# A ninth loop round that a branch ends early, and an output ring of 292 columns, in a grouped 1x1 convolution

## The chip, the cores and the metric

The kernel runs on one core of one Trainium2 chip. The metric is device time in microseconds (us) of that core, lower is better. Runs of one kernel mostly agree within 0.3%, so differences need several runs and are given here with medians, ratios and 95% intervals.

## The reference

The input `x` is 512 x 512 pixels of 192 channels in bf16, in 4 groups of 48 channels; each group is multiplied by its own 48 x 48 matrix.

```python
def reference(x, w):                       # k = 1, G = 4, Cg = 48
    xg = xp.reshape(B, H + 2 * pad, W + 2 * pad, G, Cg)
    ...
            out = out + jnp.einsum('bhwgc,gcd->bhwgd', xg[:, i:i+H, j:j+W, :, :], w[i, j])
    return out.reshape(B, H, W, C)
```

About 100.7 MB are read and 100.7 MB written, and the arithmetic per byte is small.

## The kernel before

Pixels lie along 128 partitions; a "column" is one pixel of each partition (384 bytes a partition). The SP queue loads columns into an input ring of 3 slots of 80 columns. TensorE (PE) transposes 4 columns at a time (a "group"), VectorE copies the transposed data to SBUF, PE multiplies with the block weights, ScalarE (ACT) casts the result into an output ring, and ACT's queue stores parts of that ring. Two groups make a "pair". There are 514 groups, 257 pairs.

The sizes and the cutting of the output ring into stores:

```python
RCOLS = SLOTS * BIG                  # 240
OGRID = (72, 144, 216, 288)          # where a store ends in the output ring
OCOLS = OGRID[-1]
LATE_COLS = 240                      # near the end: parts of 44 ...
LATE_PART = 44
LAST_PARTS = (12, 32, 16, 8)         # ... and these for the last stores
# cut
```

PE's program has a loop. Its body is 30 pairs, because buffer addresses and semaphores repeat after 60 groups. What does not divide by 30 is straight code ahead of the loop:

```python
def loop_spans(units):
    body, out, run = RCOLS // 4, [], []
    # cut
            first = max((run[0].g0 - 1) // 2, 1)                            # 9
            rounds, rest = divmod(run[-1].g1 - 2 * first - 2, body)         # 8, 14
            if rounds > 1:
                out.append((first + rest // 2, body // 2, rounds))          # (16, 30, 8)
# cut
            for first, body, rounds in LOOPS:
                for pair in range(pair, first):      # 16 pairs of straight code
                    step(pair)
                with pe.Fori(0, rounds):             # 8 rounds of 30 pairs
                    for pair in range(first, first + body):
                        step(pair)
                pair = first + rounds * body
            for pair in range(pair, NP):             # one pair more
                step(pair)
```

ACT copies a group into the output ring once the store that last used its columns has landed (`landed` below), and issues a store when its last group is done:

```python
            for g in range(NG):
                act.wait_ge(mm_done, g + 1)
                while todo and stores[todo[0]].g1 <= g - 1:
                    issue(todo.pop(0))
                if over[g] is not None:
                    landed(over[g])
                # cut: the copy
```

Two "special fields" of 48 columns are written to leave some of the 16 DMA engines out, or to give them less, to even out their work (in the trace of before, the load of such a transfer over 4 engines has one early semaphore update, at 84.9 us, and then four landings, at 107.9 to 110.9 us; a full load has 16):

```python
PARTIAL = (                                   # queue, first row, rows, engines, columns less
    ("sync", 0, 16, 4, 0), ("sync", 32, 16, 4, 0),
    ("pool", 52, 44, 11, 0), ("pool", 20, 12, 3, 0), ("pool", 96, 32, 8, 0),
)
UNEVEN = (("sync", 0, 16, 4, 16), *PARTIAL[1:])
FRONT = ((6, ((48, PARTIAL), (32, FULL))), (11, ((48, UNEVEN), (32, FULL))))
```

## Time and profile before

| | before |
|---|---|
| time, first three runs | 477.03 to 477.23 us, median 477.2 |
| span of the profiled run | 475.5 us |
| DMA from 32 to 436 us | 431 GB/s, share 1.00 |
| bytes moved | 201.57 MB |
| ACT's waits for stores | 17.7 us, nine times |
| PE's instruction fetches (queue q8) | 9 packets, 0.15 MB |

This is the view of windows. Each line has a stretch in us and its length, the busy time of each engine with its count of instructions, the granted PE clock, the mean busy share of the 16 DMA engines, and GB/s:

```profile
28.00:32.00 4.00, 3.97 (x63) 3.69 (x62) 2.12 (x3) 3.65 (x6) 0.00 (x0) 1.00 1.02 344
32.00:436.00 404.00, 375.20 (x5463) 339.43 (x5461) 217.74 (x228) 342.79 (x455) 11.19 (x20) 0.99 1.00 431
436.00:464.00 28.00, 26.30 (x379) 23.12 (x376) 14.99 (x16) 25.03 (x34) 0.00 (x0) 1.00 1.00 426
464.00:475.50 11.50, 0.00 (x0) 0.00 (x0) 0.00 (x0) 0.76 (x1) 0.00 (x0) 0.63 0.71 299
```

From 32 to 464 us the DMA engines have, on the average of each stretch, no free time. In that time no compute engine is busy throughout: PE has 375 us of work in 404, ACT 343. At 431 GB/s the 201.57 MB alone need 467.7 us of the 475.5 us. The last stretch still moves data, though PE is done and ACT has one copy left.

The page's lines of the DMA queues (packets, MB, share of the 16 engines' span) show where the bytes go: q1 loads, q10 stores, q0 the GpSimd transfers, q8 and q14 instructions:

```profile
q1 hardware_dynamic: 4320, 97.44, 48.0%
q10 hardware_dynamic: 4976, 97.42, 47.9%
q0 software_dynamic: 1216, 6.49, 3.3%
q8 instruction: 9, 0.15, 0.1%
q14 instruction: 9, 0.07, 0.0%
```

The source view of the loop's line shows its branches; the columns are the count and then the shortest, median and longest duration in ns:

```profile
L392 PEldq ALU_OP  x8: 36/36/42, 85.7 to 461.5; - x8
L392 PEldq COMPARE_BRANCH  x8: 76/208/239, 85.8 to 461.6; - x8
```

The view of waits shows ACT waiting for stores to leave the output ring (total us, times, longest):

```profile
ACT oring L446 <- DMA out_dram<-oring: 17.7, 9, 3.9
```

And the end of the timeline (start us, us, engine, line) shows ACT's last copy and its last two store issues; the span ends more than 10 us later:

```profile
463.58 0.34 ACTq L427 DMA_DIRECT2D out_dram<-oring  x1
463.96 0.80 ACT L446 CAST oring<-o_ps 128x768 bf16<-128x768 f32 x1 [0.28 <-issue]
464.79 0.34 ACTq L427 DMA_DIRECT2D out_dram<-oring  x1
```

### The profile page before, as it was taken

Reading aid. Unit: us, or ns where it says so; the run is one execution under the profiler, and the core shown is the slowest. Engines: PE = TensorE matmul, PEld = TensorE weight load, DVE = VectorE, ACT = ScalarE, POOL = GpSimd, SP = SyncE. Lnnn points to the kernel's source line nnn. Section 1 sums busy time; section 2 is a strip of 40 time slices with the busy share of each in tenths; the row PEclk is TensorE's granted clock in tenths of the full one; section 3 lists DMA queues with packets and bytes.
Section 4 is the critical chain, followed back from the end, with each engine's and each line's share of the span. In section 5 each row is a group of like instructions: output and inputs, shape, how many; then the busy total and the mean of one; then the engine's idle time right before and its main releaser. Section 6 shows DMA issues by size and latency. Waiting matters only on the chain.

```text
span 475.5 us, 13580 instructions
## 1 busy us (share of the span) xinstructions
PE 427.4 (90%) x6178; PEld 386.3 (81%) x6178; DVE 246.8 (52%) x258; ACT 388.9 (82%) x515; POOL 12.5 (3%) x28
## 2 busy tenths in 40 slices
PE   5999999999698999999999897999698988999990
PEld 4988888888597988888888786888697877888870
DVE  2555565555354555555555543655354554555540
ACT  2899899998587998999998795898687868998890
POOL 1000000200002000000000000200002000000000
PEclk9999999999999999999999998999989999999996
DMA  8999999999999999999999999999999999999997
GB/s 326 439 393 421 435 426 429 442 416 433 435 434 428 435 421 435 435 429 435 429 434 432 430 432 430 432 430 428 433 433 428 433 429 427 428 435 428 423 429 307
DMA packets 10530, 201.57 MB, mean 424 GB/s; under 512 B 2096, under 2 KB 2096, under 8 KB 2608
## 3 DMA queue, kind: packets, MB, share of 16 engines
q1 hardware_dynamic: 4320, 97.44, 48.0%
q10 hardware_dynamic: 4976, 97.42, 47.9%
q0 software_dynamic: 1216, 6.49, 3.3%
q8 instruction: 9, 0.15, 0.1%
q14 instruction: 9, 0.07, 0.0%
HBM read 100.68 MB, written 100.66 MB: 423 GB/s over the span
## 4 chain that ended last, share of the span: by engine, by line
PE 61%; DMA 19%; ACT 12%; another core or an unknown queue 3%; issue 2%; ACTq 1%; SPq 0%; POOLq 0%
PE o_ps L370 35%; PE xT_ps L350 26%; ACT oring L446 12%; DMA out_dram<-oring 10%; DMA ring<-in_x_dram 9%; ACTq L427 1%; SPq L320 0%; SPq L313 0%; ACTq L420 0%; POOLq L300 0%; POOLq L299 0%; ACTq L429 0%
## 5 line engine op out<-in xcount | busy, mean ns | idle before, releaser
L446 ACT CAST oring<-o_ps 128x768 bf16<-128x768 f32 x514 | 387.6, 801 | 75.1 <-PE o_ps L370 47.0
L409 DVE COPY xT_sb<-xT_ps 128x1536 bf16<-128x1536 bf16 x257 | 246.1, 958 | 211.9 <-PE xT_ps L350 211.9
L370 PE MATMUL o_ps<-wt,xT_sb 128*128 128x144 bf16 (+1 forms) x3084 | 288.4, 235 | 25.1 <-ACT oring L446 20.6
L370 PEld LDWEIGHTS o_ps<-wt,xT_sb 128*128 128x128 bf16 x3084 | 211.6, 99 | 63.3 <-ACT oring L446 55.0
L350 PE MATMUL xT_ps<-ident,ring 128*128 128x128 bf16 x3084 | 220.4, 221 | 8.4 <-POOLq L300 4.3
L350 PEld LDWEIGHTS xT_ps<-ident,ring 128*128 128x128 bf16 x3084 | 188.3, 99 | 11.3 <-POOLq L300 4.5
L286 POOL DMA_DIRECT2D fill<-in_x_dram x8 | 4.6, 573 | 350.2 <-PE xT_ps L350 231.6
L296 POOL DMA_DIRECT2D ring<-in_x_dram x6 | 3.3, 560 | 0.0
L307 POOL DMA_DIRECT2D out_dram<-oring x6 | 3.3, 556 | 0.0
L332 PE MATMUL o_ps<-w_sb,esel 48*128 48x48 bf16 x10 | 0.6, 209 | 2.6 <-DMA w_sb<-in_w_dram 2.6
L332 PEld LDWEIGHTS o_ps<-w_sb,esel 48*128 48x128 bf16 x10 | 0.4, 111 | 2.5 <-POOL esel L273 2.5
L402 DVE CAST wt<-o_ps 128x480 bf16<-128x480 f32 x1 | 0.7, 657 | 3.2 <-PE o_ps L332 3.2
L446 ACT ACT_TABLE_LOAD x1 | 1.3, 1283 | 0.8 <-PEq L466 0.8
L273 POOL TENSOR_SCALAR_AFFINE_SELECT esel<-esel 48x272 bf16<-48x272 bf16 x1 | 0.4, 402 | 0.0
L270 POOL MEMSET esel<- 48x272 bf16 x1 | 0.3, 318 | 0.3 <-POOLq L466 0.3
L277 POOL TENSOR_SCALAR_AFFINE_SELECT ident<-ident 128x128 bf16<-128x128 bf16 x1 | 0.3, 282 | 0.0
L271 POOL MEMSET ident<- 128x128 bf16 x1 | 0.2, 198 | 0.0
L466 POOL MEMSET const-float32-0.0<- 128x1 f32 x1 | 0.1, 98 | 0.3 <-issue 0.3
L466 POOL MEMSET const-bfloat16-1.0<- 128x1 bf16 x1 | 0.1, 101 | 0.0
L466 POOL MEMSET const-uint8-127<- 128x1 uint8 x1 | 0.1, 101 | 0.0
L466 POOL MEMSET const-float32-1.0<- 128x1 f32 x1 | 0.1, 98 | 0.0
## 6 DMA issues: line engine op xcount, KB each, us to landing
ring<-in_x_dram SPq DMA_DIRECT2D x22, 3840.0 KB, 29.0
out_dram<-oring ACTq DMA_DIRECT2D x21, 3456.0 KB, 42.6
out_dram<-oring ACTq DMA_DIRECT2D x3, 2112.0 KB, 20.6
out_dram<-oring ACTq DMA_DIRECT2D x3, 1536.0 KB, 34.8
ring<-in_x_dram SPq DMA_DIRECT2D x2, 1536.0 KB, 35.0
out_dram<-oring ACTq DMA_DIRECT2D x1, 3072.0 KB, 37.9
out_dram<-oring ACTq DMA_DIRECT2D x1, 2688.0 KB, 37.5
ring<-in_x_dram SPq DMA_DIRECT2D x1, 2688.0 KB, 25.4
```

Of the source, the lines that this page charges most:

```text
L273: gp.affine_select(out=esel[:], in_=esel[:], pattern=[[-1, ECOLS]], compare_op=AluOpType.is_equal, fill=0.0, base=ESHIFT, channel_multipli ...
L286: gp.dma_start(dst, src).then_inc(fill_sem[k], 16)
L296: gp.dma_start(sbuf, dram).then_inc(ld_sem[ld_key[p.i, n]], 16)
L307: gp.dma_start(dram, sbuf).then_inc(st_sem[i][n], 16)
L332: last = pe.matmul(o_ps[:, NOB - 1, col:col + CG], lhsT=esel[:, s0:s0 + 128], rhs=w_sb[:, g, :], start=True, stop=True, skip_group_check=True)
L350: last = pe.transpose(xT_ps[:, g % NXP, j * 128:(j + 1) * 128], xg[:, j * 128:(j + 1) * 128], ident[:])
L370: last = pe.matmul(o_ps[:, v % NOB, c0_:c1_], lhsT=xs[:, j * 128:(j + 1) * 128], rhs=wt[:, WOFF[tc]:WOFF[tc] + (c1_ - c0_)], start=(tc == ...
L402: dve.tensor_copy(wt[:], o_ps[:, NOB - 1, 0:WCOLS]).then_inc(wc_sem, 1)
L409: dve.tensor_copy(xT_sb[pair % NXS][:, 0:n * 2 * UC].rearrange("p (g c) -> p g c", g=n), xT_ps[:, b0:b0 + n, 0:2 * UC]).then_inc(e_done[pa ...
L427: act.dma_start(dram, sbuf).then_inc(st_sem[i][n], 16)
L446: act.copy(out_columns(g).rearrange("p (u c) -> p u c", u=2), o_ps[:, v % NOB:v % NOB + 2, 0:UC]).then_inc(fa_done[g % (2 * NTOK)] if g < ...
L466: nc = _bacc.Bacc("TRN2", target_bir_lowering=False, num_devices=1)
```

## The change

The changed kernel is called after. The intent is twofold. PE's program gets shorter: the seven pairs that do not divide by 30 are run as a ninth round of the loop, which a branch leaves after those seven. And the output ring gets 4 columns longer, with one part of 76 columns among parts of 72.

```diff
-OGRID = (72, 144, 216, 288)
+OGRID = (72, 144, 220, 292)
-LAST_PARTS = (12, 32, 16, 8)
+LAST_PARTS = (32, 16, 12, 8)
...
-                out.append((first + rest // 2, body // 2, rounds))
+                out.append((first, body // 2, rounds, rest // 2))
...
-            for first, body, rounds in LOOPS:
+            for first, body, rounds, rest in LOOPS:
                 for pair in range(pair, first):
                     step(pair)
-                with pe.Fori(0, rounds):
-                    for pair in range(first, first + body):
+                with pe.Fori(0, rounds + 1) as i:
+                    for pair in range(first, first + rest):
                         step(pair)
-                pair = first + rounds * body
+                    with pe.If(i < rounds):
+                        for pair in range(first + rest, first + body):
+                            step(pair)
+                pair = first + rounds * body + rest
```

## The prediction

> **What bounds the kernel now.** The DMA engines. By the view of windows the core moves 431 GB/s at a share of 1.00 from 32 to 436 us and 426 GB/s from 436 to 464 us. The page's 201.57 MB at 431 GB/s are 467.7 us of the 475.5 us span. The rest (about 8 us) is the start, a dip to 344 GB/s from 28 to 32 us, and the tail: ScalarE's last copy ends at 464.8 us and 10 us of stores still drain. [...]
>
> The compute engines have slack. A pair of groups takes about 1.65 us in undisturbed stretches of the timeline, so 257 pairs need about 424 us (estimate). ScalarE waits 17.7 us, nine times, for stores to free the output ring, but at a DMA share of 1.00 that only shows that bytes are queued.
>
> **What the change does.**
> 1. Loop: before, 16 pairs of straight code, 8 rounds of 30 pairs, one pair. After, 9 pairs, 8 rounds of 30, a ninth of 7 that a branch leaves, one pair: the same 257 pairs. PE's static code shrinks by 7 pairs of 48 instructions, 336 of about 2,290. Fetches were 9 packets of 16 KB (page, instruction queue q8), each about 0.94 us on one DMA engine in the trace's records; I expect 7 or 8. [...] This trace has 8 loop branches of about 0.21 us (source view), and no PE fetch after 89 us, so the 30-pair body stays resident; I expect no refetch. Added: nine branches of 0.1 to 0.25 us, hidden behind PE's slack.
> 2. Ring of 292 columns with a part of 76: 36 stores before and after, same bytes. ScalarE's 17.7 us of store waits should shrink by a few us at most; the DMA queue is full anyway, so nothing of that reaches the end.
> 3. Last parts 32, 16, 12, 8 instead of 12, 32, 16, 8: the tail is a backlog draining one store after another (the last three land at 472.2, 474.1 and 475.0 us), at the same rate in any order. Under 0.3 us.
>
> **What is left.** In the last store, the slowest DMA engine finishes 1.7 us after the median one and 0.9 us after the next. If that engine also carries PE's fetches, two fewer give at most about 0.9 us; otherwise their mean is 0.1 us. I expect part of it.
>
> **Predicted time:** 476.7 us, 8 in 10 between 475.5 and 477.7. Faster by over 2%: 0.01; within 2%: 0.97; slower by over 2%: 0.02.
>
> **What would show each step.** DMA share still 1.00 and 431 GB/s in the middle; q8 at 7 or 8 packets with none late in the run; 9 more compare-and-branches with no gap at PE around them; store waits a little shorter; a tail of about 10 us.
>
> **What would make it wrong.** [...] If the shifted stores change how the 16 DMA engines drift apart, the end moves by 1 to 2 us either way.

Three passages are cut, where marked. The forecast's sum is 477.2 us, the median of before's first three runs, less 0.5 us for the two fetches: 476.7 us. Three of its figures are estimates: 0.1 to 0.25 us for a branch (the trace of before has seven of 207 to 239 ns and one of 76 ns), under 0.3 us for the last parts, and 1 to 2 us for shifted stores (in before's last store the last engine is 0.9 us behind the next and 1.7 us behind the median).

## The result, and the profile after

| | before | after |
|---|---|---|
| median of 6 runs | 477.28 us (477.03 to 478.10) | 476.38 us (476.04 to 477.45) |
| ratio | | 0.998, interval 0.9967 to 0.9993 |
| span of the profiled run | 475.5 us | 474.6 us |

A ratio in this document is the mean time of one kernel's fast runs over the mean of the other's in the same rounds, so it is not quite the ratio of the medians. The kernel is 0.9 us faster, well within 2%, but the interval excludes 1. The predicted 476.7 us was 0.3 us too high and the range 475.5 to 477.7 us holds the result.

The lines of after that answer to those shown of before. The windows:

```profile
28.00:32.00 4.00, 3.97 (x61) 3.60 (x59) 2.39 (x3) 3.45 (x6) 0.00 (x0) 1.00 0.92 349
32.00:436.00 404.00, 375.77 (x5448) 339.27 (x5445) 217.18 (x228) 341.78 (x454) 11.17 (x20) 0.98 1.00 431
436.00:464.00 28.00, 26.02 (x375) 22.89 (x373) 15.09 (x16) 24.02 (x33) 0.00 (x0) 1.00 1.00 426
464.00:475.50 11.50, 0.59 (x6) 0.38 (x6) 0.00 (x0) 1.59 (x2) 0.00 (x0) 0.69 0.69 290
```

The middle is the same to the last digit: 431 GB/s at share 1.00, then 426. The gain is not there.

The two queues whose packets matter are q10 and q8; q0 stands between them on the page:

```profile
q10 hardware_dynamic: 4976, 97.42, 47.9%
q0 software_dynamic: 1216, 6.49, 3.3%
q8 instruction: 7, 0.11, 0.1%
```

PE's fetches went from 9 packets to 7, and the stores kept their 4976 packets. The branches, from the source views of two lines, first the loop's own and then the one that leaves the ninth round:

```profile
L393 PEldq COMPARE_BRANCH  x9: 76/208/225, 73.8 to 462.2; - x9
```

```profile
L396 PEldq COMPARE_BRANCH  x9: 77/77/208, 35.1 to 461.8; - x9
```

There are ten branches more, one of them the loop's end for the ninth round. The new ones take 77 ns (84 ns in the first two rounds) where they fall through, that is, where PE goes on with the next instruction, and 208 ns the one time they are taken. The loop's own branch jumps back seven times in before and eight times in after; its last one, of 76 ns, falls through. ACT's waits for stores, and the end:

```profile
ACT oring L450 <- DMA out_dram<-oring: 13.9, 7, 3.9
```

```profile
464.62 0.34 ACTq L431 DMA_DIRECT2D out_dram<-oring  x1
465.00 0.80 ACT L450 CAST oring<-o_ps 128x768 bf16<-128x768 f32 x1 [0.21 <-issue]
465.83 0.34 ACTq L431 DMA_DIRECT2D out_dram<-oring  x1
```

ACT waits 3.8 us less for the ring. But it finishes 1.0 us later than before (its last copy ends at 465.80 against 464.76 us), and yet the span ends 0.9 us earlier. So the end is not set by ACT: it is the tail of DMA work that got shorter.

How that tail ends can be read from the trace's semaphore updates, which no view of the page prints. Each full store's semaphore gets 16 updates at different times; they are read here as one from each DMA engine, when its share has landed. The trace doesn't name the engine. These are the 16 landings of the last store, in us from the span's start:

```
before  468.1 470.6 470.8 472.1 472.1 473.1 473.2 473.3 473.3 473.3 473.4 473.5 473.7 473.7 474.1 475.0
after   468.3 470.2 470.9 471.7 472.0 472.0 472.2 473.0 473.1 473.1 473.2 473.2 473.6 473.8 473.9 474.1
```

The mean of the 16 moves by only 0.3 us (472.7 to 472.4). The last one moves by 0.9 us, and that is the gain: before, one engine came 0.9 us behind all the others; after, none does.

### The profile page after: what moved, and what is told of

Read it like the earlier page. It is cut to its first block, busy times and chain, and to the rows that moved or that the text cites. A ratio compares the mean times of both kernels' runs of the same rounds, so it can differ in the third digit from the quotient of the medians.

```text
span 474.6 us, 13600 instructions
## 1 busy us (share of the span) xinstructions
PE 428.2 (90%) x6178; PEld 386.2 (81%) x6178; DVE 246.8 (52%) x258; ACT 388.4 (82%) x515; POOL 12.5 (3%) x28
## 3 DMA queue, kind: packets, MB, share of 16 engines
q10 hardware_dynamic: 4976, 97.42, 47.9%
## 4 chain that ended last, share of the span: by engine, by line
PE 63%; DMA 20%; ACT 10%; another core or an unknown queue 2%; issue 1%; ACTq 1%; SPq 0%; POOLq 0%
PE o_ps L371 37%; PE xT_ps L351 27%; DMA out_dram<-oring 11%; ACT oring L450 10%; DMA ring<-in_x_dram 10%; ACTq L431 1%; SPq L321 0%; SPq L314 0%; ACTq L424 0%; POOLq L301 0%; POOLq L300 0%; ACTq L433 0%
```

## The experiments

Twelve kernels ran, and before ran in the same rounds. Two theories stood at the start. Theory F: the gain is the two fetches of PE code that are no longer made, one of them from the engine that ends last. Theory S: the gain is the stores' new cutting (ring and last parts), which shifts how the engines drift apart.

### One part alone: e1_loop, e2_ringlast, e3_ring

e1_loop is after with the ring and parts of before:

```diff
-OGRID = (72, 144, 220, 292)
+OGRID = (72, 144, 216, 288)
-LAST_PARTS = (32, 16, 12, 8)
+LAST_PARTS = (12, 32, 16, 8)
```

> The loop change alone, with the old ring of 288 and the old last parts. Theory F (the gain is the two instruction fetches that PE no longer makes): 7 packets on queue q8 instead of 9, and most of the 0.9 us: 0.5 to 1.0 us faster than before. Theory S (the gain comes from the stores' new cuts, that is ring and last parts): within 0.2 us of before, though q8 has 7 packets.

e2_ringlast is before with the ring and the parts of after, and e3_ring is before with the ring alone:

```diff
-OGRID = (72, 144, 216, 288)
+OGRID = (72, 144, 220, 292)
-LAST_PARTS = (12, 32, 16, 8)        # this line in e2_ringlast only
+LAST_PARTS = (32, 16, 12, 8)
```

> The ring of 292 and the new last parts, with the old loop (16 straight pairs, 8 rounds). Theory F: within 0.2 us of before, q8 at 9 packets. Theory S: 0.5 to 1.0 us faster than before, with q8 at 9. If both parts count, each of the two runs shows about half.

> The ring of 292 alone, with the old last parts, which then need a 37th store because one of them crosses the ring's end. Theory F: within 0.2 us of before. Theory S with the ring as its cause: as e2_ringlast. Theory S with the last parts as its cause: within 0.2 us of before or slower by a few tenths (one store more).

| kernel | fetches (q8) | median us | ratio to before | interval |
|---|---|---|---|---|
| before, same rounds | 9 | 477.34 | | |
| e1_loop | 7 | 476.32 | 0.9982 | 0.9968 to 0.9996 |
| e2_ringlast | 9 | 477.03 | 0.9993 | 0.9979 to 1.0006 |
| e3_ring | 9 | 477.25 | 0.9999 | 0.9986 to 1.0013 |

The loop alone brings 1.0 us, which is all of the change's gain. The ring and parts without the loop are not clear of zero; an effect of up to 0.3 us, as e2_ringlast's median has it, can't be told from noise here. In e2_ringlast's last store one engine still lands last and alone, at 474.9 us with the next at 474.0. e3_ring shows why ring and last parts were changed together: with the old parts the new ring needs a 37th store, because one part crosses the ring's end (q10 then has 5120 packets in place of 4976). ACT's waits for stores fell to 13.0 us in e3_ring:

```profile
ACT oring L446 <- DMA out_dram<-oring: 13.0, 6, 4.0
```

That is 4.7 us less waiting than before at the same time within noise: here, with the queue full anyway, taking the wait away gained nothing. How much of the waits is the ring's doing is less clear, because they move without it too: e1_loop, with the old ring, has 15.3 us of them, e2_ringlast 16.5.

### What a fetch costs: e4_code4

Four of the eight rounds of before are unrolled ahead of the loop. The work is the same, the code is longer by 120 pairs:

```diff
-                out.append((first + rest // 2, body // 2, rounds))
+                out.append((first + rest // 2 + 4 * (body // 2), body // 2, rounds - 4))
```

> The kernel before with 4 of the 8 rounds unrolled ahead of the loop: 120 pairs of straight code more, 5,760 PE instructions, about 22 more fetches of 16 KB at about 0.95 us each on one DMA engine; nothing else changes. Theory F: q8 at about 31 packets; if they all sit on the engine that ends last, up to 21 us slower; if two engines share them, about 10 us; if all sixteen share them, 1.3 us. Theory S: no matter where they sit, they would cost less than 0.3 us, since a fetch is small beside the 201 MB.

```profile
q8 instruction: 31, 0.51, 0.4%
```

It took 480.33 us at the median, ratio 1.0064 (1.0050 to 1.0077): 3.0 us slower than before. Theory S had allowed 0.3 us. None of theory F's own figures (21, 10 or 1.3 us, for one, two or sixteen engines) fits either. The 22 fetches carry 0.36 MB, which at 431 GB/s spread over all engines would be 0.8 us. In the last store eight engines stand apart:

```
e4_code4  473.1 473.1 473.2 473.2 473.2 473.2 473.3 473.7 475.9 477.4 477.7 477.8 477.9 478.0 478.2 479.0
```

Eight land by 473.7 us, one at 475.9, seven at 477.4 or later. 31 fetches dealt out in turn to eight engines are four for seven of them and three for the eighth. That gave theory R: the fetches go round eight of the sixteen DMA engines, and the engine with most fetches sets the end. Nine fetches are then one too many: eight engines have one each, and the ninth gives one of them a second.

The packets themselves can be checked. The trace does not name a packet's engine, but in before 99.6% of the packets of 512 bytes or more that start between 32 and 436 us have another packet that starts 3 to 4 ns before their recorded end, and each of the nine fetches has one that starts 13 to 15 ns before its end. Such pairs are read here as one engine's work, and packets are linked end to start. Where two engines end within a few ns a link is ambiguous, and a chain may hop to another engine there, so a single chain is evidence and no proof. In before, the chain of packets that carries the first fetch (at 18.2 us) goes on from its end at 19.2 us and reaches the ninth (at 89.1 us); the eight fetches up to 79.9 us lie on eight different chains.

### The staircase: e5_f8, e6_f9, e7_f16, e8_f17

The form of the new loop allows any number of fetches: pairs can be moved ahead of the loop, with the ninth round shorter in return. These four are e1_loop with 3, 7, 45 and 51 such pairs:

```diff
             first = max((run[0].g0 - 1) // 2, 1)
+            first += 3                 # 7 in e6_f9, 45 in e7_f16, 51 in e8_f17
             rounds, rest = divmod(run[-1].g1 - 2 * first - 2, body)
```

> The loop change of e1_loop with 3 more pairs of straight code ahead of the loop (12 instead of 9; the ninth round leaves after 4 pairs): 8 fetches of PE code. Theory R (the fetches go round eight DMA engines in turn, so the ninth is the first that gives an engine a second one, and the end is set by the engine with most fetches): q8 at 8 packets and as fast as e1_loop, 0.8 to 1.1 us faster than before. Rival P (each fetch costs its share, about 0.14 us by e4_code4's 3.0 us for 22, wherever it sits): half of e1_loop's gain, 0.4 to 0.6 us.

> The same with 7 more pairs (16 straight pairs as before, the ninth round leaves at once, the branch stands at the head of the loop): 9 fetches. Theory R: the gain is gone, within 0.3 us of before, though the kernel has the new loop and branch. Rival B (the gain comes from the branch or the loop's new place, not from fetches): 0.7 to 1.1 us faster than before.

> The same with 45 more pairs (54 straight pairs, 6 full rounds and one that leaves): 16 fetches, two for each of eight engines. Theory R: as e6_f9 and before, within 0.4 us of before. Rival P: 7 fetches more than before, 0.9 to 1.0 us slower than before.

> The same with 51 more pairs (60 straight pairs): 17 fetches, so that one engine gets a third. Theory R: a step of 0.7 to 1.3 us between e7_f16 and this one. Rival P: 0.14 us between them, and about 1.1 us slower than before.

The lines of q8, in the order e5_f8, e6_f9, e7_f16 and e8_f17, show the counts as planned:

```profile
q8 instruction: 8, 0.13, 0.1%
```

```profile
q8 instruction: 9, 0.15, 0.1%
```

```profile
q8 instruction: 16, 0.26, 0.2%
```

```profile
q8 instruction: 17, 0.28, 0.2%
```

With the runs above (before's median was 477.34 us in e1_loop's and e4_code4's rounds, 477.17 us in these):

| fetches | most on one of 8 engines, by theory R | kernel | median us | ratio to before | interval |
|---|---|---|---|---|---|
| 7 | 1 | e1_loop | 476.32 | 0.9982 | 0.9968 to 0.9996 |
| 8 | 1 | e5_f8 | 476.51 | 0.9991 | 0.9979 to 1.0003 |
| 9 | 2 | e6_f9 | 477.28 | 1.0005 | 0.9992 to 1.0018 |
| 16 | 2 | e7_f16 | 477.60 | 1.0008 | 0.9995 to 1.0021 |
| 17 | 3 | e8_f17 | 478.49 | 1.0032 | 1.0019 to 1.0044 |
| 31 | 4 | e4_code4 | 480.33 | 1.0064 | 1.0050 to 1.0077 |

Theory R's steps are there: from 8 to 9 fetches 0.8 us, from 16 to 17 0.9 us, and from 9 to 16, seven fetches, only 0.3 us. Rival P (a like cost for each fetch) had asked for 0.14 us between 16 and 17 and 0.9 to 1.0 us between 9 and 16. e7_f16 is at the edge of what theory R gave it (within 0.4 us of before; the medians differ by 0.43 us). e6_f9 also rules out rival B: it has the new loop and its branch, and the gain is gone with nine fetches. The miss is e5_f8. Its ratio, 0.9991, should have been e1_loop's and is a gain of 0.4 us, which is what rival P asked for; its median's gain of 0.7 us lies between the two theories: one of its six runs took 478.05 us and pulls the mean, the other five lie between 476.11 and 476.79 us, below every run of e6_f9 (477.03 to 477.74 us). So e5_f8's interval doesn't exclude 1, and the step from 8 to 9 rests on the medians (the means differ by 0.6 us); the step from 16 to 17 is clean, with no run of one kernel inside the range of the other (477.30 to 478.04 and 478.27 to 479.29 us).

The last stores of the profiled runs bear on this without the medians. Theory R asks for one engine alone at the end with 9 or 17 fetches, and for none with 7, 8 or 16. The last landing comes behind the next by (us):

```
9 fetches       0.93 before   0.84 e2_ringlast   1.40 e3_ring   0.62 e6_f9
17 fetches      0.85 e8_f17
7 or 8 fetches  0.20 after    0.07 e1_loop       0.14 e9_after  0.05 e5_f8
16 fetches      0.18 e7_f16
```

In e7_f16, where eight engines should have two fetches each, eight landings come at 474.5 us or later and the other eight by 474.0. (The last three kernels below also have 7 fetches, and gaps of 0.6 to 0.8 us, but they move other work between the engines.)

The links in e8_f17 give eight chains with fetches. Each line is one chain; the times are the starts of its fetches in us:

```
chain of fetch  1:  17.0   87.6  169.7     (fetches 1, 9, 17)
chain of fetch  2:  26.2   98.8            (2, 10)
chain of fetch  3:  34.8  105.7            (3, 11)
chain of fetch  4:  43.3  118.6            (4, 12)
chain of fetch  5:  53.9  126.5            (5, 13)
chain of fetch  6:  61.3  140.4            (6, 14)
chain of fetch  7:  70.0  149.0            (7, 15)
chain of fetch  8:  78.7  161.1            (8, 16)
```

One chain has three fetches, seven have two, and every chain takes the fetches in steps of eight, which hopping chains would hardly do by chance. That is theory R's order. A second way of linking, a matching of all packets up to 200 us at once, gave the same partners for fetches 9 to 14 here and for the ninth of before, but not for 15 to 17, so the ends of those lines are less sure. That the engine with most fetches is the one that lands last was not traced; it follows from the counts and the steps. In its last store one engine lands at 476.0 us, 0.8 us behind the next.

### A try for a better version: e9_after to e12_w16

If the eight fetching engines end last, other work could be taken off them. The special fields leave rows short for chosen engines, and after's second special field cuts the 16 rows of its first transfer by 16 columns. e9_after is the changed kernel again, for comparison on the same chip; the other three change which rows are cut:

```diff
-UNEVEN = (("sync", 0, 16, 4, 16), *PARTIAL[1:])
+UNEVEN = (*PARTIAL[:4], ("pool", 96, 32, 8, 8))                               # e10_w8
+UNEVEN = (("sync", 0, 16, 4, 8), *PARTIAL[1:4], ("pool", 96, 32, 8, 4))       # e11_w4
+UNEVEN = (("sync", 0, 16, 4, 16), *PARTIAL[1:4], ("pool", 96, 32, 8, 16))     # e12_w16
```

> The changed kernel once more, on the chip of the next three, so that they can be set beside it. Both theories: 0.8 to 1.1 us faster than before, q8 at 7 packets.

> A try for a better version on top of the changed kernel. In the second special field, the rows that are cut short are no longer the 16 of the first transfer (4 engines, 16 columns) but the 32 of the last (8 engines, 8 columns). If those 8 are the engines that fetch PE's code, each loses about 0.9 us of work, as much as one fetch (estimate: 4 rows of 8 columns of 384 bytes are 12.3 KB, 0.46 us at 27 GB/s, once in, once out), and the end comes 0.3 to 0.8 us earlier than in e9_after. If they are not, or if the 4 engines that lose their relief of 1.8 us now end last, it is as slow or up to 1 us slower.

> Half of each: the first transfer's 16 rows cut by 8 columns, the last one's 32 rows by 4. Under the theory that the fetching engines end last: 0 to 0.5 us earlier than e9_after. Otherwise no difference of over 0.3 us.

> Both cuts at once, 16 columns for the first transfer's rows and 16 for the last one's: all 12 engines lose 1.8 us of work, the other four take it over (one group of columns more in all, 515, and a 37th store). If the fetching engines end last by no more than 1 us, the other four overtake them and nothing is won: within 0.5 us of e9_after.

The 27 GB/s for one engine in e10_w8's estimate are before's 431 GB/s over 16 engines (26.9). The relief of 1.8 us is the same estimate for 16 columns.

| kernel | median us | ratio to before | interval |
|---|---|---|---|
| before, same rounds | 477.33 | | |
| e9_after | 476.22 | 0.9982 | 0.9968 to 0.9996 |
| e10_w8 | 478.07 | 1.0018 | 1.0005 to 1.0032 |
| e11_w4 | 477.19 | 1.0006 | 0.9992 to 1.0020 |
| e12_w16 | 477.02 | 0.9993 | 0.9979 to 1.0007 |

e9_after repeats the result. None of the tries beats it, and all three missed what was expected of them: e10_w8 is 1.9 us slower than e9_after (up to 1 us was allowed), e11_w4 1.0 us (0.3 us), e12_w16 0.8 us (0.5 us). Taking the first transfer's whole relief away (1.8 us of work for each of its four engines, by the estimate in the expectation) costs 1.9 us, taking half away costs 1.0 us. That fits engines of that transfer that had no slack and already ended about as late as the fetching ones, but both kernels also cut the last transfer's rows, and the two changes were not run apart. e10_w8's last store agrees with that in part: two engines land at 475.2 and 475.9 us, the other fourteen by 474.0. Whether the eight engines of the last transfer are the ones that fetch stays open. e12_w16 adds a group and a store, so its 0.8 us have more than one possible cause and were not told apart.

## Why the prediction was right

**What bounds the kernel** was right: the middle of after moves 431 GB/s at share 1.00 as before. Of the four other runs whose middle was read, e1_loop, e2_ringlast and e3_ring moved 431 GB/s and e4_code4 429.

**Step 1, the loop.** Seven fetches came out, within the predicted 7 or 8, none of them after 71 us, and the branches cost no time that shows: e6_f9 has the branch and before's time. The count was off by one: ten branches more, not nine. The loop's body was not fetched again round by round. Before's 9 packets for about 2,290 instructions are one for about 254 (an estimate), so the 1,440 instructions of 30 pairs would be between five and six packets in each round. Before has 9 packets in all, the last at 89.1 us, 3 us after the first jump back. The same estimate, with the body counted once, gives 7.7, 8.2, 16.2, 17.3 and 31.6 packets for the kernels that fetched 7, 8, 16, 17 and 31.

**Step 2, the ring.** ACT's store waits fell from 17.7 to 13.9 us, "a few us at most", though part of that came without the ring (15.3 us in e1_loop), and e3_ring shows that 4.7 us less of them leave the time where it was (0.9999).

**Step 3, the last parts.** The order was never run alone. Together with the ring it is worth 0.3 us or nothing (e2_ringlast, 0.9993, not clear of 1).

**What is left.** The prediction said that two fewer fetches give at most about 0.9 us if the slowest engine also carries PE's fetches, 0.1 us otherwise, and took a part of it: 0.5 us off the 477.2 us it started from. The experiments agree with the condition: the measured gain is 0.9 us in the first comparison, 1.0 us for the loop alone and 1.1 us for the change once more. So the size was somewhat low because the prediction hedged between two cases that the trace of before could have helped to tell apart: its first and its ninth fetch are on one chain of packets, and its last store has one engine 0.9 us behind the rest. The term that was sized low is this one: 0.5 us was forecast and 0.9 us measured. There was luck in it too. The prediction did not know of theory R, that fetches go round eight engines, and so not that going from nine to eight or fewer is a step. One of the two saved fetches does most of the work; e5_f8's median, 0.2 us above e1_loop's, leaves little for the other.

The size of one step is not fully explained. A fetch packet takes 0.88 to 1.03 us in the trace of before, 0.94 us on the average of nine, and the two steps measure 0.8 and 0.9 us. But from one fetch on an engine to four, as theory R deals them out, the time rises by 4.0 us (476.32 to 480.33), 1.3 us each, so with many fetches something is added that no run here isolates. Nor is it shown why e7_f16 lies 0.3 us above e6_f9, with two fetches at most on an engine in both by theory R.

## What to carry to other kernels

In this kernel, with all DMA engines busy almost to the end (share 1.00 up to 464 us), the engine that ended last set the time, and not the mean: the last landing came 0.9 us earlier in after, the mean of the 16 only 0.3 us. In a kernel like it, look at the 16 landings of the last store before looking at bytes per second. Work that loads single engines, as by the steps and the links instruction fetches did here, can then cost by the most loaded engine, in steps (0.8 and 0.9 us here), and a queue with a 0.1% share was worth a microsecond. Waits of a compute engine on a saturated DMA queue need not be a gain to be had: 4.7 us of them went away in e3_ring for nothing (ratio 0.9999).

## What the traces show of fetches and branches

- PE's idle time that the view of waits puts down to nothing ("issue") did not grow with the fetches: 3.4 us with 31 (e4_code4) and 3.6 us with 9 (before). The end did come later: in this kernel, bound by the DMA engines, the ninth fetch cost 0.8 us (e5_f8 to e6_f9, by the medians) and the seventeenth 0.9 us (e7_f16 to e8_f17).
- Each fetch is a single packet of 16 KB. By the steps and the links, PE's went round eight DMA engines in turn, the ninth, by its chain, on the engine of the first (before: 18.2 and 89.1 us). The trace names no engine, so this is inferred.
- The loop's branch jumps back over 30 pairs seven times in before and eight in after, and no round fetched the body again (after: seven packets, the last at 70.2 us, before the first jump back at 73.8 us).
- A fetch packet of 16 KB takes 0.88 to 1.03 us in the traces of before and after. A store's packet of 27,648 bytes takes 1.03 us on the average of the 2,476 that start between 32 and 436 us in before.
- A compare-and-branch on PE takes 76 to 84 ns where it falls through and 207 to 239 ns where it is taken (before and after).
